# Zero-weight full-array matmuls in the attention loop, meant to hold the TensorE clock

## The chip, the cores and the metric

One core of a Trainium2 chip runs the whole kernel. The metric is the device time of one execution in microseconds (us); each figure is a median of several runs, but for those called one look. A "step" below is one turn of the kernel's main loop: 512 of them, 16 for each of 32 attention blocks. Where this document gives times per step or per stage, they are worked out from the start times of the instructions in the trace; a stage runs from the first exponential of its first step to that of the step after its last. The trace of a kernel is one execution of it. In the traces TensorE has one of two granted clocks, 0.50 or 1.00 of full speed (all 44 grants in the trace before): "cold" below means at 0.50, "warm" at 1.00.

## The reference, cut to what matters

```python
g = sigmoid((x * gate_w).sum(-1))
a = softmax(q @ k.T * 16**-0.5) @ v @ wo         # 32 heads of 16, 2048 tokens
b = long convolution of x with a kernel K built from A, B, C, dt (512 channels, 128 states)
return g * a + (1 - g) * b
```

The attention part needs 32 x 2048 x 2048 exponentials. The convolution part is done in chunks of 64 tokens: states per chunk (S), a scan over the 32 chunks, and outputs (y) from the states and from a small matrix within the chunk (T).

Of the kernel before, what the change touches and what calls it, by code (L numbers as in the profile page):

```python
# [11 lines left out]
P = 128  # L12
# [12 lines left out]
class Buf:  # L25


    def __init__(self, name, kind, free, dt):
        self.name, self.kind, self.free, self.dt = name, kind, free, dt
        self.t = None  # L30
        self.st = {}
        self.first = self.last = None
        self.over = ()
        self.lo = self.hi = None
        self.closed = False
# [12 lines left out]
class Prog:  # L48
# [84 lines left out]
    def op(self, eng, fn, R=(), W=(), alone=False):  # L133
        deps = self._deps(eng, R, W)
        i = self.cnt[eng]
        if i and (alone or self.alone.get(eng)):
            deps[eng] = i - 1
        self.alone[eng] = alone
        self.cnt[eng] += 1
        self._record(eng, fn, deps, eng, i, R, W)  # L140
# [49 lines left out]
class Sched:  # L190


    def __init__(self, prog):
        self.p = prog
        self.thr = []
        self.flag = {}
        self.lock = {}
        self.bud = {"PE": 0.0, "DVE": 0.0, "POOL": 0.0}

    def add(self, gen):  # L200
        self.thr.append([gen, next(gen)])
# [4 lines left out]
    def _ok(self, t, req):  # L206
        k = req[0]
        if k == "AFTER":
            return req[1] in self.flag and self.flag[req[1]] + req[2] <= self.p.q
        if k == "Q":  # L210
            return self.p.q >= req[1]
        if k == "LOCK":
            if self.lock.get(req[1]) is None:
                self.lock[req[1]] = t
                return True
            return False
        if self.bud[k] > 0:
            self.bud[k] -= req[1]
            return True
        return False  # L220

# [165 lines left out]
def build(nc, A_x, A_wqkv, A_wo, B_A_re, B_A_im, B_B_re, B_B_im, B_C_re, B_C_im, B_log_dt, B_Dskip, gate_w, out):  # L387
    ins = dict(x=A_x.flatten_outer_dims().tensor, w=A_wqkv.tensor, wo=A_wo.tensor, are=B_A_re, aim=B_A_im, bre=B_B_re,
               bim=B_B_im, cre=B_C_re, cim=B_C_im, ldt=B_log_dt.tensor, dsk=B_Dskip.tensor, gw=gate_w.tensor,
               out=out.flatten_outer_dims().tensor)  # L390
    with ExitStack() as es:
        bufs = declare(nc, es)
        prog = Prog(bufs)
        for b in bufs.values():
            b.over, b.order = (), 0
        record(nc, prog, bufs, ins)
        place(nc, bufs)
        prog = Prog(bufs)
        record(nc, prog, bufs, ins)
        prog.emit(nc, es)  # L400
# [6 lines left out]
def record(nc, p, B, ins):  # L407
# [3 lines left out]
    OA, MB = B["OA"], B["MB"]  # L411
    SC = [B[f"SC{i}"] for i in range(3)]
    sch = Sched(p)
# [4 lines left out]
    def mm(out, lhsT, rhs, R, W, start=True, stop=True, pos=None):  # L418
        kw = {} if pos is None else dict(tile_position=pos)
        op("PE", lambda t: t.matmul(out(), lhsT(), rhs(), start=start, stop=stop, skip_group_check=True, **kw), R, W)  # L420
# [44 lines left out]
    wm = B["wm"]  # L465
# [47 lines left out]
    def proj(kind, idx, c, bank):  # L513
        for q4 in range(4):
            proj_mm(kind, idx, c, bank, q4)
        proj_ev(kind, idx, c, bank)

    def mk_qm(b):
        qc, pi, w = b // 8, (b % 8) // 2, b % 2
        op("DVE", lambda v: v.tensor_scalar(Qm(512 * (b % 2), [[1, 512]]), B[f"Q{qc}"](512 * pi, [[1, 512]]),  # L520
                                            msk(w, [[1, 1]]), None, ALU.mult), [(B[f"Q{qc}"], pi), (msk, 0)], [(Qm, b % 2, b)])


    def qk(q):
        b, kt = divmod(q, 16)
        pi = (b % 8) // 2
        slots = [(SC[((4 * q + j) // 2) % 3], (4 * q + j) % 2) for j in range(4)]
        for j in range(4):
            sc, half = slots[j]
            mm(lambda sc=sc, half=half: sc(512 * half, [[1, 512]]),  # L530
               lambda j=j: KT(pi * S + 128 * kt, [[1, 128]], 32 * j, 32),
               lambda j=j: Qm(512 * (b % 2), [[1, 512]], 32 * j, 32),
               [(KT, (pi, kt // 4)), (Qm, b % 2, b)], [x + (q,) for x in (slots if j == 0 else [slots[j]])], pos=(32 * j, 0))

    def ex(h):
        sc, e = SC[h % 3], h % 7
        op("ACT", lambda a: a.activation(ET(1024 * e, [[1, 1024]]), sc(0, [[1, 1024]]), AF.Exp, scale=DH ** -0.5),  # L537
           [(sc, 0, h // 2), (sc, 1, h // 2)], [(ET, e, h)])

    def pv(q):  # L540
        b, kt = divmod(q, 16)
        pi, w = (b % 8) // 2, b % 2
        for j in range(4):
            h, e = 8 * pi + 2 * j + w, (2 * q + j // 2) % 7
            mm(lambda j=j: OA(0, [[1, 512]], 32 * j, 32), lambda h=h: VE(kt * 560 + 17 * h, [[1, 32]]),
               lambda e=e, j=j: ET(1024 * e + 512 * (j % 2), [[1, 512]]), [(VE, kt), (ET, (2 * q) % 7, 2 * q), (ET, (2 * q + 1) % 7, 2 * q + 1)],
               [(OA, 0, b)], kt == 0, kt == 15, pos=(0, 32 * j))

    def norm(b):
        qc, pi, w = b // 8, (b % 8) // 2, b % 2  # L550
        o = 0
        op("DVE", lambda v: v.transpose(OT(o, [[1, 512]]), OA(0, [[1, 512]])), [(OA, 0, b)], [(OT, 0, b)])  # L552
        op("DVE", lambda v: v.reciprocal(Rz(16 * w, [[1, 16]]), OT(o + 16, [[32, 16]])), [(OT, 0, b)], [(Rz, w)])
        op("DVE", lambda v: v.tensor_tensor(ON(16 * w, [[32, 16], [1, 16]]), OT(o, [[32, 16], [1, 16]]),
                                            Rz(16 * w, [[1, 16], [0, 16]]), ALU.mult), [(OT, 0, b), (Rz, w)], [(ON, w)])
        if w == 1:
            op("DVE", lambda v: v.transpose(OnT[qc](pi * 512, [[1, 512]]), ON(0, [[1, 512]])), [(ON, 0), (ON, 1)],
               [(OnT[qc], pi)])
# [519 lines left out]
    first = [[V(1), V(2)], [K(1)], [V(3)], [V(4)], [V(5)], [K(2), V(6)], [V(7)], [V(8)], [V(9)], [K(3)]] + [[V(k)] for k in range(10, 16)]  # L1078
# [8 lines left out]
    for q in range(NQ):  # L1087
        p.q = q
        ex(2 * q)
        if q + 1 < NQ:  # L1090
            qk(q + 1)
        ex(2 * q + 1)
        b, kt = divmod(q, 16)
        rate = dict(PE=.62 if q > 50 else 1.0, DVE=1.65, POOL=1.8)
        if b == 0:
            if q > 1:
                pv(q - 2)
        elif q == 16:
            pv(14)
            pv(15)  # L1100
        elif kt == 1:
            rate["PE"] = 1.05
        elif kt == 2:
            pv(q - 2)
            pv(q - 1)
            rate["PE"] = .2
        elif q >= 1:
            pv(q - 1)
        if kt == 0 and b >= 1:
            norm(b - 1)  # L1110
            rate["DVE"] -= 2.0
        if kt == 12 and b + 1 < 32:
            mk_qm(b + 1)
        if q < len(first):
            for w in first[q]:
                proj(*w, mb)
                rate["DVE"] -= .7
            rate["PE"] = 0
        sch.step(rate)
        if q == NQ - 1:  # L1120
            while sch.thr:
                p.q += 1
                sch.step(dict(PE=1e3, DVE=1e3, POOL=1e3))
                assert p.q < NQ + 3000, [t[1] for t in sch.thr]
# [47 lines left out]
```

## The kernel before: what the change touches

Attention runs as a loop of 512 steps. A step issues two exponentials of 128x1024 on ScalarE, the score matmuls of the next step (`qk`) and the output matmuls of the last one (`pv`), and then whatever background work (projections, S, K, y, output projection) fits a budget in microseconds per step. TensorE writes into banks of its output memory, PSUM: scores into SC, attention output into OA, background work into MB. ET holds the exponentials, VE the values.

```python
for q in range(NQ):                       # NQ = 512
    ex(2 * q)                             # exponential, reads score bank SC
    if q + 1 < NQ:
        qk(q + 1)                         # 4 matmuls, 32 rows x 128 cols each, 512 columns
    ex(2 * q + 1)
    b, kt = divmod(q, 16)
    rate = dict(PE=.62 if q > 50 else 1.0, DVE=1.65, POOL=1.8)
    ...
    elif kt == 1:
        rate["PE"] = 1.05                 # no pv: the output bank is being read
    elif kt == 2:
        pv(q - 2); pv(q - 1)
        rate["PE"] = .2
    elif q >= 1:
        pv(q - 1)                         # 4 matmuls, 128 rows x 32 cols, into the bank OA
    if kt == 0 and b >= 1:
        norm(b - 1)                       # VectorE reads OA
    ...
    sch.step(rate)                        # background work, PE budget in us
```

The y matmuls are one kind of background work, S another. One "y quarter" of a step is four matmuls Tt (weights X) and eight matmuls Py whose weights are the scan states SG.

Below, an "ordinary y step" has one y quarter and one output group of four `pv` matmuls, and a "light" step has no background work. At the start of the kernel stands `wm`, a tile of zeros, with nine matmuls on it, meant to warm up TensorE (they start from 1.2 us on; the first grant of 1.00 begins at 6.4 us).

The softmax here doesn't subtract the row's maximum and nothing guards it: scores larger than these inputs give would overflow.

## Time and profile before

1045.68 us, median of 3 runs (1043.96 to 1048.17); profiled span 1040.5 us.

| stage | loop steps | us | mean granted clock in a window within it |
|---|---|---|---|
| first seven blocks (projections, parameters) | 0 to 111 | 219.5 | 0.88 to 0.92, then 0.50 |
| S and K stage, two scans | 112 to 303 | 377.6 | 0.51 to 0.64 |
| y stage, two scans | 304 to 447 | 291.3 | 0.50 |
| output projection, without the last step | 448 to 510 | 119.9 | 0.68, then 0.56 |

The page of the kernel before shows, in this order, the busy time of the engines, the occupancy of ScalarE in 40 slices of the span (tenths), and the granted TensorE clock in the same slices (tenths of full speed):

```profile
PE 752.9 (72%) x6617; PEld 212.2 (20%) x6617; DVE 636.2 (61%) x1356; ACT 978.2 (94%) x1041; POOL 3.5 (0%) x11
...
ACT  5999999999999998999899989999999999999996
...
PEclk8988987556665556655556665555555555557756
```

ScalarE is busy for 94% and sets the pace. TensorE is at half its clock in most slices after the first seven.

The groups view of the kernel before (line, engine, operation, output from inputs, shapes, count; busy us, mean ns of one; idle us before them and what ended it):

```profile
L537 ACT ACTIVATE ET<-SC 128x1024 bf16<-128x1024 f32 x1024 | 963.9, 1110 | 40.0 <-PE SC L420 39.0
L420 PEld LDWEIGHTS MB<-Py,SG 128*32 128x32 bf16 x1024 | 42.8, 222 | 9.2 <-issue 1.3
L420 PEld LDWEIGHTS OA<-ET,VE 128*32 128x32 bf16 x2048 | 53.7, 101 | 188.6 <-issue 183.6
```

The 1024 exponentials are nearly all of ScalarE's time. The last two lines have weights of the same size, 128x32: those with 512 bytes between elements took 222 ns to load, those that are neighbours 101 ns.

The timeline of the kernel before, TensorE only, in a step without background work (start us, duration us; in brackets the idle time before and what ended it):

```profile
499.44 0.61 PE L420 MATMUL SC<-Qm,KT 32*128 32x512 bf16 x4 [0.67 <-ACT ET L537]
499.98 0.62 PE L420 MATMUL OA<-ET,VE 128*32 128x512 bf16 x4
501.27 0.61 PE L420 MATMUL SC<-Qm,KT 32*128 32x512 bf16 x4 [0.67 <-ACT ET L537]
```

and in a step with a y quarter:

```profile
861.80 0.61 PE L420 MATMUL SC<-Qm,KT 32*128 32x512 bf16 x4 [0.18 <-ACT ET L537]
862.34 0.62 PE L420 MATMUL OA<-ET,VE 128*32 128x512 bf16 x4
862.89 0.28 PE L420 MATMUL MB<-Tt,X 64*32 64x64 bf16 x4
863.10 0.47 PE L420 MATMUL MB<-Py,SG 128*32 128x64 bf16 x8
863.75 0.61 PE L420 MATMUL SC<-Qm,KT 32*128 32x512 bf16 x4 [0.18 <-ACT ET L537]
```

The first step takes 1.83 us from scores to scores, the second 1.95 us. In both it is "ACT ET" that the scores wait for, at half clock. From the start times, scores to scores: in the 103 cold steps without background work among steps 100 to 303 the median is 1.833 us, with 0.921 us between the first and the second exponential; in the 109 cold ordinary y steps it is 2.004 us, with 1.078 us between them.

### The profile page before, as it was taken

The numbers are of one execution on the slowest core, as the hardware profiler recorded it, in microseconds if no ns is written. First come the engines' busy times: TensorE is split into PE (matmuls) and PEld (weight loads), VectorE is DVE, ScalarE is ACT, GpSimd is POOL, SyncE is SP. The second block draws the span as 40 slices with busy tenths as digits, with TensorE's granted clock in tenths as the row PEclk, the third lists the DMA queues.
The fourth block names the chain that finished last, engine by engine and source line by source line (L and its number), as shares of the span: only waits on it lengthen the run. The fifth ranks groups of instructions, "written<-read, shape, count | busy, mean of one in ns | idle before, by whom it ended". The sixth has DMA issues, their size and how long they took to land.

```text
span 1040.5 us, 16316 instructions
## 1 busy us (share of the span) xinstructions
PE 752.9 (72%) x6617; PEld 212.2 (20%) x6617; DVE 636.2 (61%) x1356; ACT 978.2 (94%) x1041; POOL 3.5 (0%) x11
## 2 busy tenths in 40 slices
PE   5867667666776656766577778888868888877765
PEld 2211112111111111111111123333313333311111
DVE  7737889996567997589876530116999951031201
ACT  5999999999999998999899989999999999999996
POOL 0000000000000000000000000000000000000000
PEclk8988987556665556655556665555555555557756
DMA  8700000007876007840057663465353434100000
GB/s 177 154 9 1 1 1 1 1 1 217 207 200 182 1 0 168 221 139 1 11 142 198 187 173 89 95 141 123 92 112 90 95 90 99 37 16 26 21 6 21
DMA packets 227404, 92.17 MB, mean 89 GB/s; under 512 B 191873, under 2 KB 215041, under 8 KB 225281
## 3 DMA queue, kind: packets, MB, share of 16 engines
q1 hardware_dynamic: 225600, 90.21, 34.7%
q10 hardware_dynamic: 1728, 0.92, 0.4%
q8 instruction: 52, 0.85, 0.3%
q14 instruction: 24, 0.19, 0.1%
HBM read 27.92 MB, written 35.65 MB: 61 GB/s over the span
## 4 chain that ended last, share of the span: by engine, by line
ACT 57%; DVE 27%; PE 12%; issue 2%; SPq 1%; DMA 1%; DVEq 0%; POOL 0%; POOLq 0%
ACT ET L537 56%; PE MB L420 6%; DVE G L872 4%; PE SC L420 4%; DVE s L870 4%; DVE s L867 3%; DVE s L865 3%; DVE SG L874 3%; PE OA L420 2%; DVE VE L503 1%; DVE OT L552 1%; SPq L896 1%; DVE VE L468 1%; DVE Sst L821 1%; DVE KT L510 1%
## 5 line engine op out<-in xcount | busy, mean ns | idle before, releaser
L537 ACT ACTIVATE ET<-SC 128x1024 bf16<-128x1024 f32 x1024 | 963.9, 1110 | 40.0 <-PE SC L420 39.0
L420 PE MATMUL SC<-Qm,KT 32*128 32x512 bf16 x2048 | 288.4, 554 | 212.6 <-ACT ET L537 207.5
L420 PE MATMUL OA<-ET,VE 128*32 128x512 bf16 x2048 | 286.0, 562 | 0.1
L420 PEld LDWEIGHTS SC<-Qm,KT 32*128 32x128 bf16 x2048 | 54.6, 97 | 411.3 <-ACT ET L537 396.4
L420 PEld LDWEIGHTS OA<-ET,VE 128*32 128x32 bf16 x2048 | 53.7, 101 | 188.6 <-issue 183.6
L932 DVE CAST Yst<-MB 128x256 bf16<-128x256 f32 x32 | 13.4, 418 | 117.9 <-PE MB L420 117.9
L552 DVE STREAM_TRANSPOSE OT<-OA 128x512 f32<-128x512 f32 x32 | 24.0, 751 | 73.8 <-PE OA L420 73.6
L821 DVE CAST Sst<-MB 128x256 bf16<-128x256 f32 x64 | 27.0, 422 | 62.4 <-PE MB L420 55.0
L562 DVE TENSOR_TENSOR tt<-B,D 128x1024 bf16<-128x1024 bf16 x96 | 62.0, 687 | 1.3
L420 PE MATMUL MB<-Py,SG 128*32 128x64 bf16 x1024 | 59.8, 314 | 1.2 <-issue 1.2
L420 PE MATMUL MB<-Qt,X 64*32 64x256 bf16 x512 | 39.3, 398 | 27.2 <-DVE Sst L823 22.1
L872 DVE TENSOR_TENSOR G<-s,s 128x256 f32<-128x256 f32 x120 | 54.3, 452 | 4.1
L870 DVE TENSOR_TENSOR s<-s,SG 128x256 f32<-128x256 f32 x120 | 53.5, 446 | 0.0
L867 DVE TENSOR_TENSOR s<-G,MU 128x256 f32<-128x256 f32 x120 | 52.7, 439 | 0.0
L865 DVE TENSOR_TENSOR s<-G,MU 128x256 f32<-128x256 f32 x120 | 50.7, 422 | 0.1
L420 PEld LDWEIGHTS MB<-Py,SG 128*32 128x32 bf16 x1024 | 42.8, 222 | 9.2 <-issue 1.3
L1021 DVE SCALAR_TENSOR_TENSOR fo<-MB,g,Yl 128x512 bf16<-128x512 f32 x13 | 9.7, 747 | 55.2 <-PE MB L420 55.2
L420 PE MATMUL MB<-Tt,X 64*32 64x64 bf16 x512 | 35.7, 268 | 8.5 <-DVE Yst L932 8.4
L874 DVE CAST SG<-G 128x256 bf16<-128x256 f32 x120 | 35.5, 295 | 4.1
L562 DVE TENSOR_TENSOR PT<-tt,tt 128x1024 bf16<-128x1024 bf16 x48 | 33.2, 692 | 1.6
L562 DVE TENSOR_TENSOR ft<-FP,L 128x1024 f32<-128x1024 f32 (+1 forms) x32 | 33.7, 1085 | 0.4
L420 PEld LDWEIGHTS MB<-Tt,X 64*32 64x32 bf16 x512 | 19.0, 136 | 63.1 <-issue 62.8
(115 smaller groups left out, 415.7 us busy)
## 6 DMA issues: line engine op xcount, KB each, us to landing
gm_ptd<-PT SPq DMA_DIRECT2D x16, 1024.0 KB, 5.0
Py<-gm_ptd SPq DMA_DIRECT2D x32, 512.0 KB, 4.4
gm_sd<-Sst SPq DMA_DIRECT2D x64, 128.0 KB, 2.3
gm_kpd<-Kst SPq DMA_DIRECT2D x16, 256.0 KB, 3.5
Tt<-gm_kpd SPq DMA_DIRECT2D x128, 32.0 KB, 3.4
gm_xrd<-in_A_x_dram SPq DMA_DIRECT2D x1, 2048.0 KB, 13.1
X<-gm_xrd SPq DMA_DIRECT2D x8, 256.0 KB, 4.7
gm_ytd<-Yst SPq DMA_DIRECT2D x32, 64.0 KB, 1.8
```

The lines of the kernel that those rows point to most:

```text
L420: op("PE", lambda t: t.matmul(out(), lhsT(), rhs(), start=start, stop=stop, skip_group_check=True, **kw), R, W)
L468: op("DVE", lambda v: v.memset(VE(0, [[1, 16 * 560]]), 1.0), [], [(VE, k) for k in range(16)])
L537: op("ACT", lambda a: a.activation(ET(1024 * e, [[1, 1024]]), sc(0, [[1, 1024]]), AF.Exp, scale=DH ** -0.5), [(sc, 0, h // 2), (sc, 1, h / ...
L552: op("DVE", lambda v: v.transpose(OT(o, [[1, 512]]), OA(0, [[1, 512]])), [(OA, 0, b)], [(OT, 0, b)])
L562: op(eng, lambda v: v.tensor_tensor(o(), a(), b_(), f), R, W)
L821: op("DVE", lambda v, bank=bank: v.tensor_copy(Sst(512 * bank, [[256, 2], [1, 128]]), MB(0, [[256, 2], [1, 128]])), [(MB, 0, ('S', blk, ba ...
L865: op(e, lambda v: v.tensor_tensor(s2(0, [[128, 2], [1, 128]]), G(0, [[128, 2], [1, 128]]), MU(d0, [[0, 2], [1, 128]]), ALU.mult), key("G", ...
L867: op(e, lambda v: v.tensor_tensor(s3(0, [[128, 2], [1, 128]]), G(128, [[-128, 2], [1, 128]]), MU(D + d0, [[D, 2], [1, 128]]), ALU.mult), k ...
L870: op(e, lambda v, so=so: v.tensor_tensor(s2(0, [[1, 256]]), s2(0, [[1, 256]]), sg(so, [[1, 256]]), ALU.add), [(s2, 0)] + ks, [(s2, 0)])
L872: op(e, lambda v: v.tensor_tensor(G(0, [[1, 256]]), s2(0, [[1, 256]]), s3(0, [[1, 256]]), ALU.add), [(s2, 0), (s3, 0)], [(G, 0)])
L874: op(e, lambda v, so=so: v.tensor_copy(sg(so, [[1, 256]]), G(0, [[1, 256]])), key("G"), ks)
L932: op("DVE", lambda v: v.tensor_copy(Yst(r2 * 256, [[1, 256]]), MB(0, [[1, 256]])), ky, [(Yst, r2, u)])
```

## The change

The intent: let TensorE do useless work where it has time, so that the higher clock is granted for longer. The added matmuls have zero weights and zero data, use the full 128x128 array and 512 columns, and add their zeros to the output bank OA, which is open for accumulation (or to MB in the second step of a block). How many follow a step is worked out from what the scheduler has spent: two for nothing, one for a y quarter (.65) or an S bank (.6), none for more. Two more stand ahead of each block's last output matmuls.

```diff
+    def keep(b, n, bank=None):
+        o, tag = bank or (OA, b)
+        for _ in range(n):
+            mm(lambda: o(0, [[1, 512]]), lambda: wm(0, [[1, P]]), lambda: wm(0, [[1, 512]]), [(wm, 0)], [(o, 0, tag)],
+               bank is not None, bank is not None)
...
         elif q == 16:
+            keep(0, 2)
             pv(14)
...
         elif q >= 1:
+            if kt == 0:
+                keep(b - 1, 2)
             pv(q - 1)
...
+        sch.spent = 0.0
         sch.step(rate)
+        idle = max(0, round((.95 - sch.spent) / .43)) if q >= len(first) else 0
+        if kt == 1 and sch.lock.get("MB") is None:
+            keep(b, idle, (MB, "warm"))
+        elif kt > 1:
+            keep(b, idle)
```

(`spent` sums the PE budget that background work took in the step; cut here.) Below, one such matmul is called a "keep".

More of the change, by code (lines that the diff above doesn't have):

```diff
@@ L198, in __init__ @@
         self.bud = {"PE": 0.0, "DVE": 0.0, "POOL": 0.0}
+        self.spent = 0.0
     def add(self, gen):
@@ L218, in _ok @@
             self.bud[k] -= req[1]
+            if k == "PE":
+                self.spent += req[1]
             return True
```

## The prediction

> **What bounds it now.** ScalarE. The page gives ACT 94% busy, nearly all of it the 1024 exponentials of 128x1024 that read the score banks (963.9 us). In the timeline a step (two exponentials) takes 1.83 us where TensorE does only scores and attention output. 1024 exponentials at 0.915 us, plus the head (first at 20 us) and tail, are about 968 us; the other 78 us are (a) about 53 us of stalls over 0.25 us each, mostly "PE SC" waits behind a MB eviction, and (b) about 25 us of small delays, 19 us of them in the y stage (620 to 910 us), where a step takes 1.95 us. The granted clock is 0.61 on average and 0.50 in nearly the whole y stage (windows view).
>
> **What the change is for.** It adds 128x128x512 matmuls on zeros (2 in steps without other work, 1 in steps with one y quarter or S bank) to keep the clock up. [...] all grants last multiples of 3.41 us. Counting streamed columns per window, the clock rises after windows with more than 0.72 to 0.73 of the time streaming and falls after warm windows with less than about 0.37, with one or two exceptions: about 3000 columns a window.
>
> **Costed.** Group start to group start, cold: scores 0.53, output 0.54, Tt 0.20, Py 0.40; a full matmul 0.54 alone, 0.43 more for a second. Warm: 0.31, 0.33, 0.18, 0.45, 0.31, 0.22.
> - Light steps, 2 keeps: 2048 columns in 1.83 us, 3800 a window: warm from about 180 us on. But they were already 1.83 us cold; no gain in themselves.
> - S/K stage (240 to 620 us): warm. The nine stalls of about 1.42 us (two S banks in one step, with an eviction between) should shrink to a few tenths: -10 us. Two stalls of 3.7 us behind VectorE's scan stay.
> - y stage: a step is 1.95 us not because TensorE is slow: scores start 55 ns after the exponential ends, and the first exponential's distance to the second is 1.05 instead of 0.92 us while Tt/Py matmuls run. Warm steps at 617 to 622 us show the same or worse (2.0 to 2.1). So warmth gains little here. With 1 keep, 1728 columns in 1.95 us are 3020 a window: on the edge. Once cold, the chain 0.53+0.54+0.20+0.40+0.54 = 2.21 us makes TensorE the bound, its share of streaming 0.65 stays under 0.72, and only a light step rewarms. About 105 such steps, two thirds cold, at +0.26 us, and ten block starts with two keeps: +25 us.
> - Output projection: stalls of 1.26 us shrink: -2 us. Zero matmuls into MB at step 1 of a block may wait for evictions, and the two ahead of a block's last output delay its normalization: +2 us.
>
> **Prediction.** 1058 us, range 1030 to 1082. Faster by over 2%: 0.10; within 2%: 0.55; slower by over 2%: 0.35.
>
> **What would show it.** Granted clock 0.9 to 1.0 in 180 to 620 us and in 920 to 1030 us; 1.42 us stalls mostly gone; y stage with a mixed clock (0.6 to 0.75), cold steps of about 2.2 us where exponentials wait for "PE SC", longer than 290 us in total; light steps still 1.83 us.
>
> **What would make it wrong.** If the y stage stays warm (the edge is within a few per cent), nothing is lost there and the result is about 1035 or below; if exponentials also speed up in warm y steps, below 1025. If zero matmuls slow exponentials, or waits of keeps on evictions pile up, it is slower, above 1080.

What stands there of grants and windows was read from the trace before. In it 43 of the 44 grants last 1 to 93 times 3.41 us, and the end of the execution cuts the last one. A "window" here and below is one stretch of 3.41 us, counted from the start of the first grant. Counted again, 512 columns are taken as 0.216 us at full clock (median from start to start of 49 pairs of `MB<-Wv,xT` matmuls) and as twice that at half clock. By the prediction's count, none of 212 cold windows under 0.72 was followed by a warm one, and 21 of 23 over it were; of 21 warm windows under 0.37 one was followed by a warm one, and of 47 over it 45. These are counts of one execution; what grants the clock they do not show.

## More of the kernel before

SG is stored as [33 chunks][real, imaginary][128 channels], so that 32 weights of one channel lie 256 elements, or 512 bytes, apart:

```python
mm(lambda q=q, j=j: MB(64 * q, [[1, 64]], 32 * j, 32),
   lambda ri=ri, i=i: sg(ri * 128 + CB * bl + 16 * hf + i, [[256, 32]]),   # weights
   lambda ri=ri, i=i: Py(r * YN + ri * 16 * T + i * T, [[1, T]]), ...)     # 64 columns
```

## The result, and the profile after

1052.57 us (1051.1 to 1054.0, 4 runs) against 1044.91 us (1043.96 to 1048.17, 4 runs): ratio 1.0073, 95% interval 1.0049 to 1.0098. The profiled span grew from 1040.5 to 1050.4 us, which is more than the 7.7 us between the medians: the profiled execution of the kernel before was a fast one (other executions of it had spans of up to 1046.6 us).

The page after:

```profile
PE 786.9 (75%) x7232; PEld 246.0 (23%) x7232; DVE 636.3 (61%) x1356; ACT 985.3 (94%) x1041; POOL 3.5 (0%) x11
...
PEclk7989998699999998989899989777998667889999
```

The clock did what was wanted: its mean rose from 0.615 to 0.896. ScalarE is as busy as before, and the time did not fall. By stage, from the exponentials:

| loop steps | before, us | after, us | difference |
|---|---|---|---|
| 0 to 111 | 219.5 | 221.7 | +2.2 |
| 112 to 303 | 377.6 | 376.6 | -1.0 |
| 304 to 447 (y stage) | 291.3 | 302.2 | +10.9 |
| 448 to 510 | 119.9 | 117.6 | -2.3 |

Only the third difference is clear. Kernels that have no keep in a stage, and the same schedule there, differ among themselves from profile to profile: 219.5 to 223.5 us in steps 0 to 111, 377.3 to 378.5 us in steps 112 to 303 and 116.7 to 120.1 us in steps 448 to 510 (before and the runs sg_contig, sg_stride128 and blk below).

The windows view over three stretches (us from the span's start; busy time and count of PE, PEld, DVE, ACT and POOL; then granted clock, DMA share, GB/s), before:

```profile
240.00:340.00 100.00, 67.72 (x620) 15.93 (x612) 68.80 (x141) 94.90 (x104) 0.62 (x2) 0.64 0.73 194
620.00:910.00 290.00, 242.03 (x2672) 92.15 (x2672) 142.84 (x373) 283.16 (x288) 0.62 (x2) 0.50 0.42 96
910.00:985.00 75.00, 57.04 (x359) 11.97 (x355) 18.44 (x40) 71.26 (x78) 0.00 (x0) 0.68 0.07 22
```

and after:

```profile
240.00:340.00 100.00, 69.38 (x699) 20.11 (x696) 67.61 (x137) 96.44 (x106) 0.62 (x2) 0.98 0.76 206
620.00:910.00 290.00, 246.04 (x2751) 101.10 (x2747) 142.84 (x372) 278.24 (x278) 0.62 (x2) 0.83 0.42 95
910.00:985.00 75.00, 56.08 (x444) 14.92 (x440) 18.46 (x42) 74.08 (x81) 0.00 (x0) 0.91 0.08 20
```

In the middle stretch the clock rose from 0.50 to 0.83, and yet ScalarE got through 278 instructions instead of 288. In the two others it got through two and three more.

The groups after:

```profile
L540 ACT ACTIVATE ET<-SC 128x1024 bf16<-128x1024 f32 x1024 | 971.0, 1164 | 43.0 <-PE SC L423 37.8
L423 PE MATMUL OA<-wm 128*128 128x512 bf16 x609 | 223.6, 423 | 0.0
L423 PEld LDWEIGHTS MB<-Py,SG 128*32 128x32 bf16 x1024 | 42.8, 222 | 7.6 <-issue 1.5
```

There are 609 keeps in OA (and 6 in MB), 0 us of idle ahead of them. The loads of SG still take 222 ns.

Two y steps after, the first while the clock was high, the second while it was low (timeline, TensorE only):

```profile
641.58 0.40 PE L423 MATMUL SC<-Qm,KT 32*128 32x512 bf16 x4 [0.42 <-ACT ET L540]
641.91 0.40 PE L423 MATMUL OA<-ET,VE 128*32 128x512 bf16 x4
642.24 0.26 PE L423 MATMUL MB<-Tt,X 64*32 64x64 bf16 x4
642.43 0.45 PE L423 MATMUL MB<-Py,SG 128*32 128x64 bf16 x8
642.81 0.39 PE L423 MATMUL OA<-wm 128*128 128x512 bf16 x1
643.61 0.40 PE L423 MATMUL SC<-Qm,KT 32*128 32x512 bf16 x4 [0.41 <-ACT ET L540]
```

```profile
679.79 0.61 PE L423 MATMUL SC<-Qm,KT 32*128 32x512 bf16 x4
680.34 0.62 PE L423 MATMUL OA<-ET,VE 128*32 128x512 bf16 x4
680.88 0.28 PE L423 MATMUL MB<-Tt,X 64*32 64x64 bf16 x4
681.09 0.47 PE L423 MATMUL MB<-Py,SG 128*32 128x64 bf16 x8
681.49 0.61 PE L423 MATMUL OA<-wm 128*128 128x512 bf16 x1
682.03 0.61 PE L423 MATMUL SC<-Qm,KT 32*128 32x512 bf16 x4
```

The warm step takes 2.03 us and TensorE still waits 0.41 us for ScalarE: a fast TensorE gains nothing here. The cold step takes 2.24 us and has no bracket: now TensorE is the bound, and the keep (0.54 us from its start to the scores) is what made it so. Over the whole y stage, the ordinary y steps ("mixed" ones saw both clocks; the last column is the pair of exponentials that runs during the step's matmuls):

| | cold: number, median us | mixed | warm: number, median us | first to second exponential, cold / warm |
|---|---|---|---|---|
| before | 109, 2.004 | 0 | 1, 2.035 | 1.078 / 1.133 us |
| after | 30, 2.240 | 12, 2.017 | 68, 1.990 | 1.081 / 1.078 us |

So 30 steps lost 0.24 us each (7 us), and 68 warm ones gained practically nothing. Most of the rest of the y stage's loss lies in light and two-output steps that turned cold: 2.06 and 2.49 us, with two keeps, where some 1.8 us was usual.

In the S stage two things nearly cancel. Nine steps with two S banks took 3.26 us before, because the second bank waits for VectorE to empty MB (in one of them, at 395.49 us, TensorE had been idle for 0.93 us when `DVE Sst` released it); after, seven of them were warm and took 2.41 us, which gives back 6 us. All 163 warm steps of the stage together gave back 9.8 us, from scores to scores. But 13 cold steps took 4.3 us more than before, and 16 in which the clock changed 4.8 us more. One place where this happens: TensorE waits 4.39 us for VectorE, the clock falls from 1.00 to 0.50 during the wait (the grant of 0.50 runs from 390.9 to 401.2 us), and a keep of 0.54 us stands ahead of the scores that ScalarE is waiting for:

```profile
393.56 0.65 PE L423 MATMUL MB<-Qt,X 64*32 64x256 bf16 x8 [4.39 <-DVE Sst L832]
394.14 0.61 PE L423 MATMUL OA<-wm 128*128 128x512 bf16 x1
394.68 0.61 PE L423 MATMUL SC<-Qm,KT 32*128 32x512 bf16 x4
```

This stop of ScalarE, one of two that follow a scan on VectorE, cost 3.7 us before and 4.6 us after (excess over 0.915 us between two exponentials); the other grew from 3.7 to 3.9 us.

### The profile page after: what moved, and what is told of

It reads as the page before. It is cut to its first block, busy times and chain, and to the rows that moved or that the text cites. A ratio compares the mean times of both kernels' runs of the same rounds, so it can differ in the third digit from the quotient of the medians.

```text
span 1050.4 us, 17545 instructions
## 1 busy us (share of the span) xinstructions
PE 786.9 (75%) x7232; PEld 246.0 (23%) x7232; DVE 636.3 (61%) x1356; ACT 985.3 (94%) x1041; POOL 3.5 (0%) x11
## 4 chain that ended last, share of the span: by engine, by line
ACT 49%; DVE 23%; PE 23%; issue 2%; SPq 1%; DMA 1%; DVEq 0%; POOL 0%; POOLq 0%
ACT ET L540 49%; PE OA L423 9%; PE MB L423 7%; PE SC L423 6%; DVE G L881 4%; DVE s L879 3%; DVE s L876 3%; DVE s L874 3%; DVE SG L883 2%; DVE OT L561 1%; DVE VE L506 1%; DVE VE L471 1%; SPq L905 1%; DVE Sst L830 1%; DVE Sst L832 1%
## 5 line engine op out<-in xcount | busy, mean ns | idle before, releaser
L423 PE MATMUL SC<-Qm,KT 32*128 32x512 bf16 x2048 | 222.5, 424 | 181.2 <-ACT ET L540 178.5
L423 PE MATMUL OA<-wm 128*128 128x512 bf16 x609 | 223.6, 423 | 0.0
L423 PE MATMUL OA<-ET,VE 128*32 128x512 bf16 x2048 | 218.2, 428 | 0.0
L423 PEld LDWEIGHTS OA<-ET,VE 128*32 128x32 bf16 x2048 | 50.8, 95 | 134.6 <-issue 133.1
L423 PEld LDWEIGHTS OA<-wm 128*128 128x128 bf16 x609 | 43.6, 99 | 75.7 <-issue 70.7
L423 PE MATMUL MB<-Qt,X 64*32 64x256 bf16 x512 | 31.1, 322 | 32.4 <-DVE Sst L832 27.8
```

Source lines behind the costliest of these rows:

```text
L423: op("PE", lambda t: t.matmul(out(), lhsT(), rhs(), start=start, stop=stop, skip_group_check=True, **kw), R, W)
```

## The experiments

Twelve kernels ran. All were right except two. Loop steps 304 to 447 are the y stage.

Theory A: in y steps ScalarE itself is slow, because its exponentials are held up while the small matmuls run, whatever the clock; the change loses where such a step is cold and carries a keep. Rival B: the keeps cost time everywhere. Rival C: the warm y steps did gain, and the loss is elsewhere.

### 1. No keeps in the y stage (y_none)

```diff
+        if 304 <= p.q < 448:
+            return
         o, tag = bank or (OA, b)
```

> No zero matmuls in loop steps 304 to 447 (the y stage), all others as in the change. Theory A (a y step is set by ScalarE, whose exponentials are slowed while the Tt and Py matmuls run, at either clock; the change loses where a y step is cold and carries a keep): the y stage takes 291 to 294 us again instead of 302 to 303, at a clock near 0.50, and the kernel about 1042 us, ratio to before 0.993 to 1.001. Rival B (the zeros cost time everywhere, or slow the exponentials in all stages): still over 1047 us, and the y stage gets back less than half of its 11 us. Rival C (the warm y steps gained, and the loss is elsewhere): the y stage is 302 us or more.

Measured: 1045.67 us (6 runs), before 1045.86 (11 runs), ratio 1.0004 (0.998 to 1.0028). The y stage took 292.0 us, 108 of its 110 ordinary y steps were cold at 2.009 us. That undoes the whole loss of the y stage (302.2 to 292.0) and speaks against B and C. It also shows that the keeps outside the y stage are worth next to nothing as they stand: the total is that of before. (It lies 4 us over the 1042 us expected, but within the ratio expected, up to 1.001.)

### 2. Two keeps in y steps (y_two)

```diff
+        if 304 <= q < 448 and idle == 1:
+            idle = 2
         if kt == 1 and sch.lock.get("MB") is None:
```

> Two zero matmuls instead of one in the y stage's steps of one y quarter, about 2240 columns a step and so over 3800 a window of 3.41 us. Theory A: the y stage stays warm (clock over 0.93), hardly any cold step of 2.24 us is left, warm y steps still take 1.97 to 2.01 us, the stage 289 to 295 us; total about 1041 us, ratio 0.991 to 1.001. Rival C (a y step is set by the cold TensorE, so a stage that is warm throughout gains): y steps 1.83 to 1.88 us, stage under 278 us, total under 1028 us. Rival B (zeros slow the exponentials): warm y steps over 2.05 us and a total over 1050 us.

Measured: 1050.89 us (1045.13 to 1053.49), ratio 1.0043 (1.0019 to 1.0067). The windows view of this run over the y stage:

```profile
622.00:917.00 295.00, 249.21 (x2917) 105.66 (x2956) 145.17 (x377) 285.25 (x288) 0.62 (x2) 0.95 0.42 96
```

The clock is 0.95, 102 of 110 ordinary y steps are warm, and they take 1.999 us, with 1.083 us between first and second exponential. This is the clearest answer to rival C: with the y stage warm nearly throughout, its steps are as long as cold ones without a keep. The y stage took 295.2 us, 4 us over before, in a few cold steps with two keeps (2.67 us). The total was about 10 us above what theory A expected, and just over the 1050 us at which rival B was to be seen; B's other mark, warm y steps over 2.05 us, did not come. The profiled run lost 5.5 us more than the change itself in steps 112 to 303, where the two kernels have the same schedule: there the profiles of three kernels with one schedule (after, y_none, y_two) gave 376.6, 376.9 and 382.1 us. Why this stage differs so from run to run was not shown, and that miss is not settled further.

### 3. Keeps only after steps with no background work (light_only)

```diff
+        if sch.spent > 0:
+            idle = 0
         if kt == 1 and sch.lock.get("MB") is None:
```

> Zero matmuls after the step only where the step had no other work from the scheduler (the pairs ahead of a block's last output stay). Theory A: no y step carries a keep after its work, so the y stage is 291 to 296 us, mostly cold; the S stage stays warm in most windows since light steps lie between, and the waits of about 3.2 us in steps with two S banks stay near 2.4 us; total 1038 to 1044 us. Rival B: total above 1047 us, as the light steps carry most of the keeps.

Measured: 1048.48 us (1046.44 to 1050.99), ratio 1.0028 (1.0007 to 1.0049), which is 4 us above the range expected and above rival B's mark of 1047 us. The stages tell against B all the same: steps 112 to 303 took 373.0 us, 4.6 us less than before, with most of the steps with two S banks near 2.4 us, as expected. But the y stage took 297.8 us. Most of that is due to the pairs ahead of a block's last output, which this edit leaves in: eight of the nine block starts there were cold and took 2.66 us instead of some 2.0, over 5 us in all. The light steps that were cold lost too (six at 2.06 us, and five with two output groups at 2.49 us). So even a keep in a step with nothing else to do costs time when it falls into a cold stretch. Steps 448 to 510 took 121.0 us, which is too near the spread of this stage to be read.

### 4. Weights of the Py matmuls read as neighbours (sg_contig, wrong result)

```diff
-                           lambda ri=ri, i=i: sg(ri * 128 + CB * bl + 16 * hf + i, [[256, 32]]),
+                           lambda ri=ri, i=i: sg(ri * 128 + 32 * (i // 4), [[1, 32]]),
```

This is the kernel before, without any keep. It asks what holds up the exponentials in y steps.

> The kernel before, with one change that makes the result wrong on purpose: the weights of the Py matmuls are read as 32 neighbours instead of 32 elements 512 bytes apart. If it is these strided weight loads that slow the exponentials, weight loads fall from 222 to about 100 ns, the distance of the first to the second exponential in y steps falls from 1.08 to about 0.92 us, y steps from 2.00 to about 1.84 us and the total to about 1030 us. If it is the matmuls as such (their PSUM writes or their number), the distance stays at 1.05 to 1.1 us and the total within 0.5% of before.

Measured: 1025.2 us (4 runs), ratio 0.98 (0.9777 to 0.9823). The y stage fell from 291.3 to 270.1 us at a clock of 0.50; 110 ordinary y steps took 1.833 us, with 0.920 us between first and second exponential. Exactly the light step's numbers, with the number of matmuls, their columns and their PSUM bank unchanged. The groups view of this run:

```profile
L537 ACT ACTIVATE ET<-SC 128x1024 bf16<-128x1024 f32 x1024 | 944.5, 1101 | 43.3 <-PE SC L420 42.3
L420 PEld LDWEIGHTS MB<-Py,SG 128*32 128x32 bf16 x1024 | 17.8, 107 | 9.1 <-issue 1.1
```

ScalarE's busy time fell by 19 us though nothing of ScalarE was edited. The trace shows the same on VectorE: the scan's two 128x256 additions took 474 and 479 ns on average in the y stage of the kernel before and 419 and 425 ns in this run, which is what they take in both kernels before the y stage. Nothing of VectorE was edited either.

### 5. A right kernel with neighbouring weights (sg_layout), and the keeps on it (sg_after, sg_keep)

The chunk index is moved innermost, by another order of the stores into the scratch tensor. The scan on VectorE then reads and writes single elements 128 bytes apart (the text on record says 64, which is a slip).

```diff
-sd.dram((CB * blk + 8 * bank) * 8192, [[256, P], [4 * 8192, 2], [1, 256]])
+sd.dram(CB * blk * 8192 + (8 * bank + 4 * pp) * 256, [[256, 4], [8192, 32], [1, 256]])     # one store for each pp
...
-tensor_copy(sg(so, [[1, 256]]), G(0, [[1, 256]]))
+tensor_copy(sg(so, [[32, 2], [64, 128]]), G(0, [[128, 2], [1, 128]]))
...
-sg(ri * 128 + CB * bl + 16 * hf + i, [[256, 32]])
+sg(31 + 64 * (CB * bl + 16 * hf + i) + 32 * ri, [[1, 32]])
```

> The kernel before with a right result and contiguous Py weights: the scan states are stored with the chunk index innermost, by another order of the stores into the scratch tensor; the scan's VectorE reads and writes become strided by 64 bytes instead. If weight loads with 512 bytes between elements are what slows the exponentials and VectorE's strided access does not, y steps take 1.83 us, the stage about 270 us instead of 291, total 1022 to 1030 us. If strided access by any engine slows ScalarE, the scan steps (near 345, 470, 720 to 845 us) get slower and the gain is under 10 us.

> The same new layout under the full change. With y steps of 1.83 us instead of 1.99 us, one keep gives 1728 columns in 1.83 us, about 3220 a window, which should hold the clock in the y stage (over 0.95) with few cold steps. Theory A: y stage 270 to 276 us, nothing lost to cold steps; total within 6 us of the new layout without keeps. If the keeps cost by themselves, total 8 us or more above it.

> The new layout, and zero matmuls only outside the y stage, and before it only after steps with no other work. Theory A: what the change gains in the S and K stage (about 4 us) and in the output stage (about 2 us) adds to the layout's gain: total 4 to 7 us under the new layout alone, about 1019 us. Rival B: no lower than the new layout alone.

Measured: 1092.21, 1098.1 and 1091.25 us, ratios 1.0443, 1.0507 and 1.0442. Ordinary y steps took 1.833 us as foretold, but the totals were missed: 1022 to 1030 us had been expected for sg_layout and about 1019 us for sg_keep. The scan's cast became far slower on VectorE (before: 295 ns), and its addition that reads SG took 593 instead of 446 ns:

```profile
L877 DVE CAST SG<-G 128x256 bf16<-128x256 f32 x120 | 89.0, 742 | 4.1
```

The scans overran their budget, and the loop waited for VectorE after each of the first two (12.7 us more than before in steps 176 to 191 and again in 240 to 255; 41 us more in all of steps 112 to 303). The y stage, with the two other scans, took 298.9 us. The layout was the wrong cure. In its presence the full change still cost 6 us more than the layout alone, and sg_keep was no lower than the layout, as rival B had it; with such stops in the way this says little of the keeps.

### 6. A middle distance (sg_stride128, wrong result)

```diff
+                           lambda ri=ri, i=i: sg(ri * 128 + 32 * (i // 4), [[64, 32]]),
```

> The kernel before with Py weights read 128 bytes apart instead of 512 (wrong result on purpose). If any stride slows the exponentials: first-to-second distance in y steps stays near 1.08 us. If it takes a wide stride: 0.92 us, as with neighbours, and y steps of 1.83 us. A value between says that it is graded.

Measured, one look: 1023.67 us. Ordinary y steps took 1.833 us with 0.921 us between the exponentials. So weights 128 bytes apart did not hold up ScalarE here, and those 512 bytes apart did (1.078 us between the exponentials, before). No other distance was tried: where between them it begins, and whether it is distance as such or certain multiples, stays open.

### 7. A right kernel with weights 128 bytes apart (blk), and the keeps on it (blk_after, blk_keep)

SG becomes four blocks of [33 chunks][real, imaginary][32 channels]. Weights lie 64 elements apart, VectorE has runs of 32 neighbours, the loads from the scratch tensor keep their form.

```diff
-sg(256 + CB * bl, [[128, 64], [1, CB]])
+sg(2112 * bl + 64, [[CB, 64], [1, CB]])
...
-so = 256 * (c + 1)
+so = 64 * (c + 1)
...
-tensor_copy(sg(so, [[1, 256]]), G(0, [[1, 256]]))
+tensor_copy(sg(so, [[32, 2], [2112, 4], [1, 32]]), G(0, [[128, 2], [32, 4], [1, 32]]))
...
-sg(ri * 128 + CB * bl + 16 * hf + i, [[256, 32]])
+sg(2112 * bl + 32 * ri + 16 * hf + i, [[64, 32]])
```

`blk_after` adds the full change. `blk_keep` adds it outside the y stage only, and before the y stage only after steps without other work (the edits of 1 and 3 together).

> The kernel before with the scan states laid out per block of 32 channels, so that the Py weights lie 128 bytes apart; VectorE still reads and writes runs of 32 neighbours, stores and loads are as before, the result is right. If wide weight strides are what slows ScalarE in y steps and VectorE keeps its speed on such runs (cast near 0.30 us, not 0.74): y steps 1.83 us, y stage about 271 us instead of 291, other stages unchanged, total 1023 to 1028 us. If VectorE is slower on these runs, its scans overrun and the total is above 1040 us.

> This layout under the full change. Theory A: y steps are now long on slack, a keep gives 3220 columns a window in warm steps of 1.83 us, but after each stall the step with a keep is cold at about 2.07 us until a light step; the y stage takes 273 to 280 us, total 0 to 10 us above the layout alone. Rival C (the change was only held back by slow y steps): 3 us or more below the layout alone.

> This layout with zero matmuls only outside the y stage, and before it only after steps with no other work. Theory A: the S and K stage gains about 4.5 us as in the run with light steps only, the output stage about 2 us; total 4 to 7 us below the layout alone, about 1019 us, the lowest of all kernels. Rival B: no lower than the layout alone.

Measured, all right, in the same rounds (before: 1045.93 us, 11 runs):

| kernel | median us | ratio to before, 95% interval | y stage, us |
|---|---|---|---|
| blk | 1025.48 | 0.9806 (0.9787 to 0.9825) | 271.3 |
| blk_after | 1037.11 | 0.99 (0.9869 to 0.9931) | 285.8 |
| blk_keep | 1019.56 | 0.9744 (0.9722 to 0.9766) | 271.3 |

The groups view of blk:

```profile
L874 DVE CAST SG<-G 128x256 bf16<-128x256 f32 x120 | 35.2, 294 | 4.1
L420 PEld LDWEIGHTS MB<-Py,SG 128*32 128x32 bf16 x1024 | 33.7, 183 | 9.2 <-issue 1.2
```

VectorE keeps its speed (294 ns), ordinary y steps take 1.833 us with 0.921 us between exponentials at a clock of 0.50, and the kernel is 2% faster (whether by over 2% the interval leaves open). A weight load still takes 183 ns, against 107 ns for neighbours, and yet ScalarE is not held up: it is hardly the length of the loads as such (in experiment 8 loads of 194 ns on average, 512 bytes apart, do hold it up; with the neighbours of block 14 counted in, the 208 loads there took 163 ns).

On this layout the full change costs 10 us by the means of the fast runs (12 us by the medians; a run of 1048.06 us is counted as slow and left out of the ratio). That is the upper end of the 0 to 10 us expected, and the y stage is longer than the 273 to 280 us expected. In its profile 37 ordinary y steps were cold at 2.167 us, 66 were warm at 1.833 us, 7 mixed. So the keep in y steps loses in the same way when y steps are short. Put only outside the y stage, and before it only after steps without other work, the keeps gain 6 us by the medians over blk alone, as foretold. In the profiles 4 us of it come in steps 112 to 303 (374.3 against 378.5 us); the 2 us expected of the output stage are not seen (117.6 against 116.7 us). blk_keep beats both kernels.

### 8. The suspected cost by itself (alone)

```diff
         sch.step(rate)
+        if kt > 2 and b in (10, 14):
+            for i in range(8):
+                mm(lambda i=i: OA(0, [[1, 64]], 32 * (i % 4), 32),
+                   lambda i=i, b=b: KT(i, [[256, 32]]) if b == 10 else KT(32 * i, [[1, 32]]),
+                   lambda: wm(0, [[1, 64]]), ..., False, False, pos=(0, 32 * (i % 4)))
```

> The suspected cost by itself, far from the y stage. The kernel before gets eight small matmuls (128x32 weights taken from the keys, 64 moving columns of zeros, added to the open output bank, so the result stays right) in each step from the fourth of attention blocks 10 and 14, whose other work is only scores and output: steps 163 to 175 read the weights 512 bytes apart, steps 227 to 239 as neighbours. Before, both stretches take 1.833 us a step with 0.921 us between first and second exponential. If wide weight strides slow ScalarE wherever they stand: block 10 goes to 1.95 to 2.02 us a step and 1.05 to 1.1 us, block 14 stays at 1.83 and 0.92 us. If it is only the y stage's operands or its PSUM bank: both stay at 1.83 us. If it is the number of small matmuls: both rise alike.

Measured, one look: 1045.4 us, before 1044.2. The timeline of this run in block 10 (weights 512 bytes apart):

```profile
346.22 0.61 PE L420 MATMUL SC<-Qm,KT 32*128 32x512 bf16 x4 [0.66 <-ACT ET L537]
346.77 0.62 PE L420 MATMUL OA<-ET,VE 128*32 128x512 bf16 x4
347.17 0.35 PE L420 MATMUL OA<-wm,KT 128*32 128x64 bf16 x8
348.08 0.61 PE L420 MATMUL SC<-Qm,KT 32*128 32x512 bf16 x4 [0.56 <-ACT ET L537]
```

and in block 14 (neighbours):

```profile
475.14 0.61 PE L420 MATMUL SC<-Qm,KT 32*128 32x512 bf16 x4 [0.56 <-ACT ET L537]
475.68 0.62 PE L420 MATMUL OA<-ET,VE 128*32 128x512 bf16 x4
476.08 0.32 PE L420 MATMUL OA<-wm,KT 128*32 128x64 bf16 x8
476.97 0.61 PE L420 MATMUL SC<-Qm,KT 32*128 32x512 bf16 x4 [0.57 <-ACT ET L537]
```

In both, TensorE has over half a microsecond to spare, and it is ScalarE that ends the wait. Over 13 steps each, the median is 1.950 us with wide weights and 1.833 us with neighbours; between first and second exponential stand 1.020 and 0.921 us (1.05 to 1.1 was expected of the first). These are other weights, zero data and another PSUM bank, so it is the distance between the loaded weights that slowed ScalarE here (1.950 against 1.833 us a step), not anything of the y stage. Why it does so, no run here shows.

## Why the prediction was right or wrong

The time, 1052.57 us against 1058 (1030 to 1082), and the most likely class, within 2%, were right. The range also holds the time of the kernel before, so the number alone tests little. Point by point:

- **ScalarE is the bound, light steps gain nothing.** Right: warm light steps after took 1.833 us, as cold ones before.
- **A warm y step gains little.** Right, and shown from both sides: 68 warm steps at 1.990 us after, 102 at 1.999 us with two keeps, 2.004 us before. The prediction named the time in which Tt and Py run as the place; the runs showed that it is the wide weight loads of Py (1.833 us a step with neighbours, sg_contig, against 2.004 us before; why those hold up ScalarE stays open).
- **A cold y step with a keep takes 2.21 us.** Right: 2.24 us.
- **The y stage costs 25 us.** Wrong in size: +10.9 us. The failed term is "two thirds cold": of the 110 ordinary y steps 30 were cold, 12 mixed and 68 warm, and the clock was 0.83 where 0.6 to 0.75 was predicted. The prediction counted streamed columns and put a warm y step "on the edge" of the boundary that it had read from the trace (after a warm window under 0.37 the clock mostly fell). In the profile after, 15 warm windows of the y stage had a share of 0.32 to 0.37 by that count, and 14 of them were followed by a warm one, while of seven such windows before, none in the y stage, one was. That count takes four small matmuls side by side as one. Counted instead as the time in which at least one matmul streams its columns, so that those which start one after another each count, the same boundary separates the windows of both profiles: of the warm windows under 0.37 none of 17 before and 2 of 24 after were followed by a warm one, and of those over it 46 of 51 and 215 of 218.
- **The S and K stage gains 10 us.** Wrong in size: -1.0 us. The steps with two S banks shrank by 0.85 us rather than by over 1.1, in seven of nine cases, and the prediction took the stage as warm throughout: the cold steps and those in which the clock changed took 9.1 us more, nearly all that the warm ones gave back. After four idle stretches of TensorE, of 2.35 to 4.39 us (ended at 250.82, 393.56, 518.59 and 614.30 us, the last three by VectorE), the clock stood at 0.50, and a keep of 0.54 us came ahead of the scores. "Two stalls of 3.7 us stay" was wrong of the first, which grew to 4.6 us. The run with keeps after light steps only got 4.6 us here.
- **The output stage gains 2 us.** Not settled: -2.3 us in the two profiles, but kernels without keeps there differ by 3.4 us in this stage, and blk_keep got none of it against blk.
- **Keeps at block starts cost 2 us.** Not measured by an experiment of its own. In the profile after, the 30 block starts from step 32 on took 2.6 us more than before, 1.7 us of it in the y stage; the waits that the prediction named are not separated. The first seven blocks took 2.2 us more, 0.8 us of it before the first keep, in a stretch (steps 0 to 15) that took 33.0 to 36.4 us in the profiles.
- The two errors of size have opposite signs and partly cancel (25 - 10 predicted, 10.9 - 1.0 measured). That the total came out close is in this part luck.

The traces also show where the time of a cold keep goes. At half clock 0.54 us pass from the start of one group of 512 columns to the next where the tiling changes (scores to output before: 376 pairs, median 0.542 us), and 0.40 us where it doesn't: between two output groups (before, 24 pairs, 0.404 us) and between two keeps (after, 23 pairs, 0.400 us). So, by the difference, the change of tiling goes with some 0.14 us of the 0.54 us of a cold keep between tiled groups, and a second keep adds 0.40 us (the prediction had 0.43); most of what makes a keep in a full step dear is the 0.40 us that its 512 columns take at half clock (0.226 us at full clock, 177 pairs after).

## What to carry to other kernels

Before buying clock for TensorE, check in the timeline whether TensorE waits for another engine in the slow steps: a higher clock can be had (0.61 to 0.90 here) and still be worth nothing, and the filler that buys it can turn into the bound where the clock drops (cold y steps of 2.24 us with a keep, 2.004 us without). If an engine's own instructions get longer in one stage, look at what the other engines read there: matmul weights 512 bytes apart cost 19 us of ScalarE's busy time in this kernel (963.9 us in its exponentials before, 944.5 us with neighbours), and a layout with 128 bytes between them took the y stage from 291.3 to 271.3 us. Filler work belongs in steps that have time for it even at the low clock, and not ahead of work that a stalled engine is waiting for: two cold keeps make a light step 2.06 us, one would fit into 1.83 us (an estimate from 0.53 us for the scores, 0.54 us for the output and 0.54 us for the keep), and no run here tried that.

## What the runs show of the hardware, in numbers

- Eight 128x32 weight loads with 512 bytes between elements raised a step's two exponentials from 1.833 to 1.950 us by themselves (run alone), and the same loads of neighbours did not (1.833 us). In the y stage a step took 2.004 us with such loads (before) against 1.833 us with neighbours (sg_contig), and VectorE's scan additions 474 to 479 ns against 419 to 425 ns. In these runs TensorE's weight reads, 512 bytes apart, slowed ScalarE and VectorE.
- A load of 128x32 weights took 107 ns on average for neighbours (sg_contig; 101 ns for those of the output matmuls before), 183 ns at 128 bytes (blk) and 222 ns at 512 bytes (before). At 512 bytes, and not at 128, ScalarE was slower too: 1.078 against 0.921 us between the exponentials.
- Counting the time in which at least one matmul streams columns (from start times, columns and granted clock, with 0.216 us for 512 columns at full clock and twice that at half), before: none of 208 cold windows under 0.72 was followed by a warm one and 21 of 27 over it were; of 17 warm windows under 0.37 none was followed by a warm one, and of 51 over it 46. After: none of 33 cold windows under 0.72 and 24 of 31 over it turned warm; 2 of 24 warm windows under 0.37 and 215 of 218 over it were followed by a warm one. After, 49 of the 50 grants last 1 to 25 times 3.41 us; the last is cut by the end of the execution.
- The 128x256 cast of VectorE took 742 ns where it wrote single bf16 elements 128 bytes apart (sg_layout), and 294 ns in runs of 32 neighbours (blk).
